# Windowed attention with a gated MLP behind it: q and k transposed on VectorE, scores as two 32-row products, one PSUM ring, and an instruction order written by a planner

## The chip, the cores and the metric

The kernel runs on one core of one Trainium2 chip. The metric is the device time of one launch in microseconds. Of the kernel before, three runs are known: 249.41, 250.86 and 250.92 us, median 250.86 us. The profile is of one execution, whose span from the first to the last instruction is 249.3 us.

## What is computed

Eight batches, eight heads, 576 tokens, 64 numbers a head, all fp32. Each token attends to itself and the 63 before it; the heads of a token laid side by side make a row of 512, which goes through a gated MLP whose gate is mixed over the tokens.

```python
scores = scale * np.matmul(q, k.transpose(0, 1, 3, 2))       # scale = 1/8
mask = (rel >= 0) & (rel < 64)                               # rel = query - key position
attn = softmax(np.where(mask, scores, -1e9))
x = np.matmul(attn, v)                                       # heads side by side: (8, 576, 512)
h = np.maximum(x @ w_in, 0.0)                                # w_in (512, 1024)
u, v = h[..., :512], h[..., 512:]
v_n = (v - mean(v)) / np.sqrt(var(v) + 1e-06)                # over the 512
v_s = np.einsum('ts,bsd->btd', w_spatial, v_n) + b_spatial   # over the 576 tokens
out = (u * v_s) @ w_out                                      # w_out (512, 512)
```

## The kernel before

**Stages of a batch.** Inputs are loaded as fp32 with the tokens on the partitions, in four chunks of 128 tokens and one of 64 (`load_heads`, `load_rem`, `load_chunk`, lines 68 to 76), so each descriptor moves one head's row of 256 bytes. GpSimd turns them into fp16 (lines 81 to 88; for batch 0 ScalarE and VectorE help) and copies v once more, shifted by 64 tokens (lines 93 to 106), so that any window of 128 keys starts on partition 0.

Attention goes in five steps `s` a batch: four pairs of heads over the tokens 0 to 511, and a fifth for the last 64 tokens of all heads ("the remainder"). In each:

- T (`emit_T`, lines 210 to 225): eight transposes on TensorE bring q and k of the pair to "numbers on the partitions", and VectorE copies the 128x1024 result from PSUM to `qk`.
- S (`emit_S`, lines 242 to 256): 16 matmuls make the scores, keys on the partitions, 64 keys against up to 192 queries. A head fills 64 rows of the array and 64 keys fill 64 columns, so four such tiles lie side by side in the array.
- E (`emit_E`, lines 264 to 270): ScalarE takes the exponential of 128x1024 scores, VectorE clips with the mask (a minimum with 0 or 65504).
- P (`emit_P`, lines 281 to 290): two matmuls with ones give the sums of the weights, 16 matmuls the products with v, both into `oz`.
- N (`emit_N1`, `emit_N2`, lines 298 to 308): ScalarE takes Ln and Exp(-x) of the sums, VectorE multiplies, which gives `x`, already transposed for the MLP.

The MLP of a batch has five units each of V (`emit_V`, lines 330 to 336: four matmuls of 512 columns, Relu on ScalarE, statistics on VectorE), U (lines 362 to 372), G (lines 382 to 394, the token mixing, five matmuls each) and O (lines 403 to 407: matmuls, a copy on ScalarE, a store), and one LN (lines 343 to 352) between V and G. The fifth unit of each is for the last 64 tokens; for V and O it takes as many matmuls of 512 columns as a full one (`pv_4`, `po_4`), in 64 of the array's 128 columns.

**PSUM** (eight banks): `tp` one bank, `sc` two, `oz` two, `mm` three for all MLP units.

**Order.** Every engine works its instructions strictly in program order, and the program order is written out by hand. `att_step` emits T of the next step, some MLP units, S of this step, P of the step before, then E and N with MLP units in between. A batch's attention runs beside the MLP of the batch before it; the lists `st[0]` to `st[4]` say which units go with which step. Batch 0 has no MLP beside it, and `warm` (line 114) fills TensorE with 16 and then four and three idle products at a time. The MLP of the last batch has no attention beside it. Loads go out on SyncE's queue one batch ahead, stores too from batch 2 on, in the same queue. The weights are loaded on GpSimd's queue, which turns them into fp16 on the way (lines 186 to 197).

Of the kernel before, what the change touches and what calls it, by code (L numbers as in the profile page):

```python
# [15 lines left out]
BIG = 65504.0  # L16


@with_exitstack
def kernel(  # L20
# [25 lines left out]
    inpool = ctx.enter_context(tc.tile_pool(name="inp", bufs=1))  # L46
    apool = ctx.enter_context(tc.tile_pool(name="attw", bufs=1))
    xpool = ctx.enter_context(tc.tile_pool(name="xt", bufs=1))
    mpool = ctx.enter_context(tc.tile_pool(name="moe", bufs=1))
# [3 lines left out]
    NAT = {}  # L53
    F16 = {}

    def new_batch(b):
        NAT[b] = [inpool.tile([128, 5, 8, 64], f32, tag=f"n{x}", bufs=2, name=f"n{x}{b}")
                  for x in "qkv"]

    def new_half(b):  # L60
        F16[b] = [inpool.tile([128, 5, 8, 64], f16, tag=f"h{x}", bufs=2, name=f"h{x}{b}")
                  for x in ("q", "k", "v", "s")]

    SRC = (q, k, v)

    def load_heads(b, x, h0, eng):
        for h in (h0, h0 + 1):
            eng.dma_start(NAT[b][x][:, 0:4, h, :],  # L68
                          SRC[x][b, h, 0:512, :].rearrange("(c p) d -> p c d", p=128))

    def load_rem(b, x, eng):
        eng.dma_start(NAT[b][x][0:64, 4, :, :], SRC[x][b, :, 512:576, :].transpose([1, 0, 2]))

    def load_chunk(b, x, c):
        sn = 128 if c < 4 else 64
        nc.sync.dma_start(NAT[b][x][0:sn, c, :, :],
                          SRC[x][b, :, 128 * c:128 * c + sn, :].transpose([1, 0, 2]))

    def cast_pair(b, x, p, eng):
        hs = slice(2 * p, 2 * p + 2)  # L80
        eng.tensor_copy(F16[b][x][:, 0:4, hs, :], NAT[b][x][:, 0:4, hs, :])  # L81

    def cast_rem(b, x, eng):
        eng.tensor_copy(F16[b][x][0:64, 4, :, :], NAT[b][x][0:64, 4, :, :])

    def cast_chunk(b, x, c, eng):
        sn = 128 if c < 4 else 64
        eng.tensor_copy(F16[b][x][0:sn, c, :, :], NAT[b][x][0:sn, c, :, :])  # L88

    def shift_pair(b, p, eng):  # L90
        hs = slice(2 * p, 2 * p + 2)
        vn, vs = F16[b][2], F16[b][3]
        eng.tensor_copy(vs[0:64, 0:4, hs, :], vn[0:64, 0:4, hs, :])
        eng.tensor_copy(vs[64:128, 1:5, hs, :], vn[64:128, 0:4, hs, :])

    def shift_rem(b, eng):
        eng.tensor_copy(F16[b][3][0:64, 4, :, :], F16[b][2][0:64, 4, :, :])

    def shift_half(b, half, eng):
        vn, vs = F16[b][2], F16[b][3]  # L100
        c = 2 * half
        if half < 2:
            eng.tensor_copy(vs[0:64, c:c + 2, :, :], vn[0:64, c:c + 2, :, :])
            eng.tensor_copy(vs[64:128, c + 1:c + 3, :, :], vn[64:128, c:c + 2, :, :])
        else:
            eng.tensor_copy(vs[0:64, 4, :, :], vn[0:64, 4, :, :])

    scratch = cpool.tile([128, 512], f16, name="scratch")
    nc.vector.memset(scratch[:], 0.0)  # L109

    def warm(n):
        t = psp.tile([128, 512], f32, tag="mm", bufs=3, name=f"warm{nc.next_id()}")
        for _ in range(n):
            nc.tensor.matmul(t[:, :], scratch[:, 0:128], scratch[:, :], start=True, stop=True)  # L114

    def load_by_pairs(b):
        new_batch(b)
        for p in range(4):
            for x in (1, 0, 2):
                load_heads(b, x, 2 * p, nc.scalar if (b == 0 and p < 2 and x == 2) else nc.sync)  # L120
        for x in (1, 0, 2):
            load_rem(b, x, nc.sync)
# [441 lines left out]
```

## Time and profile before

| | |
|---|---|
| runs | 249.41, 250.86, 250.92 us (median 250.86) |
| span of the profiled execution | 249.3 us, 0.1 us below the fastest run and 1.6 below the median |
| TensorE busy | 227.3 us, 91%, 2588 matmuls |
| VectorE, ScalarE, GpSimd busy | 155.3, 152.2, 122.1 us |
| mean granted TensorE clock | 0.962 of full speed |
| loads and stores | 40.41 MB, 120014 packets, 113776 of them under 512 bytes |

The page's slices cut the span into 40 parts of 6.2 us and give the busy share in tenths. The stage table gives for stretches of the span the busy microseconds of each engine (with the number of instructions), the granted clock, the busy share of the DMA engines and GB/s. In the timeline the columns are start, duration, engine, line, operation, tiles written and read, shapes and count, and in brackets how long the engine had been idle and for what. A matmul's duration includes the time to run through the array: the next one starts earlier, so prices below are taken from start to start. Line numbers are those of the code above.

### The profile page before, as it was taken

To read this page: it belongs to the slowest core of one execution; us is meant where nothing else is said; L and a number is where in the kernel's file an instruction comes from. 1 tells how busy PE (TensorE), PEld (TensorE's weight loads), DVE (VectorE), ACT (ScalarE), POOL (GpSimd) and SP (SyncE) were. 2 spreads that over 40 slices of the span, in tenths; PEclk is the share of its full clock that TensorE was granted. 3 is DMA by queue.
4 is the path that set the end of the run, shared out by engine and by line. 5 is a ranking of instruction groups with operands and counts; after the bars stand their busy time and mean duration, and the time that the engine had idled before them with its cause. 6 is when DMAs were issued, how large, how long until landed. Compare 5 with 4: busy or idle time off the path is not lost.

```text
span 249.3 us, 6391 instructions
## 1 busy us (share of the span) xinstructions
PE 227.3 (91%) x2588; PEld 116.8 (47%) x2588; DVE 155.3 (62%) x317; ACT 152.2 (61%) x266; POOL 122.1 (49%) x183
## 2 busy tenths in 40 slices
PE   7784996996399999999999999999999999999893
PEld 3442453553254464436544554455445544553351
DVE  6453277562459782887479556966597659755630
ACT  3373484446447666766785577756776677767423
POOL 3469638875499695369016592469135900000000
PEclk9999799799569999999999999999999999999998
DMA  8999999999999996992389948995499040014005
GB/s 159 218 184 208 216 204 229 191 201 276 249 199 210 198 178 175 246 206 52 128 192 211 192 128 221 189 198 135 137 216 156 27 165 5 3 42 149 0 3 189
DMA packets 120014, 40.41 MB, mean 162 GB/s; under 512 B 113776, under 2 KB 114864, under 8 KB 119984
## 3 DMA queue, kind: packets, MB, share of 16 engines
q1 hardware_dynamic: 114720, 34.88, 70.1%
q0 software_dynamic: 1840, 2.24, 5.2%
q10 hardware_dynamic: 3424, 2.88, 4.1%
q8 instruction: 20, 0.33, 0.6%
q14 instruction: 10, 0.08, 0.1%
HBM read 32.79 MB, written 9.44 MB: 169 GB/s over the span
## 4 chain that ended last, share of the span: by engine, by line
PE 60%; DVE 13%; ACT 9%; DMA 8%; SPq 3%; POOL 2%; issue 2%; ACTq 1%; POOLq 0%
SPq L68 3%; DMA nv_80<-in_v_dram 2%; DMA out_dram<-ob_0_1033 2%; DMA out_dram<-ob_1_3433 2%; DMA nq_78<-in_q_dram 2%; ACTq L407 1%; PE ps_0_804 L382 1%; PE warm_583 L114 1%; PE pv_0_1308 L330 1%; PE ps_0_4590 L382 1%; PE ps_0_4237 L382 1%; DVE mv_172 L336 1%; PE ps_0_3720 L382 1%; PE ps_1_895 L382 0%; PE ps_3_4653 L382 0%
## 5 line engine op out<-in xcount | busy, mean ns | idle before, releaser
L88 POOL CAST hq_2281<-nq_2285 128x512 f16<-128x512 f32 (+1 forms) x5 | 3.2, 635 | 12.8 <-DMA nq_2285<-in_q_dram 12.8
L114 PEld LDWEIGHTS <-scratch 128*128 128x128 f16 x51 | 5.0, 112 | 7.3 <-issue 3.8
L88 POOL CAST hq_3389<-nq_3393 128x512 f16<-128x512 f32 (+1 forms) x5 | 3.9, 797 | 8.8 <-DMA nq_3393<-in_q_dram 8.8
L281 PEld LDWEIGHTS <-onesK 128*64 128x64 f16 x80 | 4.6, 107 | 7.5 <-issue 5.2
L88 POOL CAST hq_2835<-nq_2839 128x512 f16<-128x512 f32 (+1 forms) x5 | 3.6, 720 | 8.3 <-DMA nq_2839<-in_q_dram 8.3
L176 ACT CAST hk_109<-nk_79 128x512 f16<-128x512 f32 x4 | 2.5, 618 | 7.5 <-DMA nk_79<-in_k_dram 7.5
L114 PE MATMUL warm_113<-scratch 128*128 128x512 f16 x16 | 5.5, 524 | 1.3 <-DVE scratch L109 1.3
L81 POOL CAST hv_110<-nv_80 128x512 f16<-128x512 f32 x4 | 2.5, 632 | 8.3 <-DMA nv_80<-in_v_dram 7.3
L88 POOL CAST hv_1729<-nv_1733 128x512 f16<-128x512 f32 (+1 forms) x5 | 3.5, 708 | 4.4 <-DMA nv_1733<-in_v_dram 4.4
L88 POOL CAST hq_1727<-nq_1731 128x512 f16<-128x512 f32 (+1 forms) x5 | 2.9, 609 | 4.6 <-DMA nq_1731<-in_q_dram 4.6
L88 POOL CAST hv_2283<-nv_2287 128x512 f16<-128x512 f32 (+1 forms) x5 | 3.2, 637 | 3.8 <-DMA nv_2287<-in_v_dram 3.8
L81 POOL CAST hv_433<-nv_437 128x512 f16<-128x512 f32 x4 | 2.5, 613 | 5.2 <-DMA nv_437<-in_v_dram 5.1
L88 POOL CAST hv_1184<-nv_764 128x512 f16<-128x512 f32 (+1 forms) x5 | 3.1, 611 | 3.9 <-DMA nv_764<-in_v_dram 3.9
L362 PEld LDWEIGHTS <-win_181 128*128 128x128 f16 x32 | 3.1, 98 | 3.8
L362 PEld LDWEIGHTS <-win_182 128*128 128x128 f16 x32 | 3.1, 98 | 3.8
L88 POOL CAST hv_1220<-nv_1224 128x512 f16<-128x512 f32 (+1 forms) x5 | 3.9, 780 | 2.0 <-DMA nv_1224<-in_v_dram 2.0
L88 POOL CAST hq_1182<-nq_762 128x512 f16<-128x512 f32 (+1 forms) x5 | 3.3, 654 | 3.2 <-DMA nq_762<-in_q_dram 2.7
L81 DVE CAST hq_108<-nq_78 128x512 f16<-128x512 f32 x4 | 1.7, 432 | 4.8 <-DMA nq_78<-in_q_dram 4.8
L281 PE MATMUL oz_3_1153<-e_1_3_1108,onesK 128*64 128x512 f16 x2 | 0.6, 611 | 4.4 <-DVE x_2_1133 L308 4.4
L88 POOL CAST hv_3391<-nv_3395 128x512 f16<-128x512 f32 (+1 forms) x5 | 3.0, 611 | 2.8 <-DMA nv_3395<-in_v_dram 2.8
L88 POOL CAST hv_2837<-nv_2841 128x512 f16<-128x512 f32 (+1 forms) x5 | 3.3, 666 | 2.0 <-DMA nv_2841<-in_v_dram 1.8
L264 ACT ACTIVATE e_1_0_831<-sc_0_813 128x1024 f16<-128x1024 f32 x1 | 1.0, 1023 | 5.2 <-PE sc_0_813 L242 5.2
(1871 smaller groups left out, 940.3 us busy)
## 6 DMA issues: line engine op xcount, KB each, us to landing
nk_79<-in_k_dram SPq DMA_DIRECT2D x9, 128.0 KB, 3.9
nq_78<-in_q_dram SPq DMA_DIRECT2D x9, 128.0 KB, 4.1
nk_436<-in_k_dram SPq DMA_DIRECT2D x9, 128.0 KB, 4.8
nq_435<-in_q_dram SPq DMA_DIRECT2D x9, 128.0 KB, 4.8
nv_437<-in_v_dram SPq DMA_DIRECT2D x9, 128.0 KB, 4.1
nk_763<-in_k_dram SPq DMA_DIRECT2D x4, 256.0 KB, 5.5
nq_762<-in_q_dram SPq DMA_DIRECT2D x4, 256.0 KB, 5.7
nv_764<-in_v_dram SPq DMA_DIRECT2D x4, 256.0 KB, 6.0
```

The source lines that it names most:

```text
L68: eng.dma_start(NAT[b][x][:, 0:4, h, :], SRC[x][b, h, 0:512, :].rearrange("(c p) d -> p c d", p=128))
L81: eng.tensor_copy(F16[b][x][:, 0:4, hs, :], NAT[b][x][:, 0:4, hs, :])
L88: eng.tensor_copy(F16[b][x][0:sn, c, :, :], NAT[b][x][0:sn, c, :, :])
L114: nc.tensor.matmul(t[:, :], scratch[:, 0:128], scratch[:, :], start=True, stop=True)
L176: nc.scalar.copy(o, i)
L264: nc.scalar.activation(e2[:, :, :], sc[:, :, :], AF.Exp, bias=0.0, scale=0.125)
L281: nc.tensor.matmul(oz[64 * h:64 * h + 64, 1, 0:n], onesK[:, :], e2[:, h, 0:n], start=True, stop=True)
L330: nc.tensor.matmul(pv[0:jn, :], xcol(b, r, j), w_in_sb[r][:, 512:1024], start=(r == 0), stop=(r == 3))
L336: nc.vector.bn_aggr(mv_t[b % NSB][0:jn, j, :], st6[0:jn, 0:6])
L362: nc.tensor.matmul(pu[:, :], w_in_sb[r][:, 128 * m:128 * m + 128], X[b, r][:, :], start=(r == 0), stop=(r == 3))
L382: nc.tensor.matmul(ps[:, :], VN[b, kk][0:kn, 128 * m:128 * m + 128], wspT[kk][0:kn, 0:512], start=(kk == 0), stop=(kk == 4))
L407: (nc.scalar if b < 2 else nc.sync).dma_start(out[b, 128 * j:128 * j + jn, :], ob[0:jn, :])
```

## The change

The kernel is rewritten around a list of steps with costs. What is computed stays the same.

- **q and k.** One contiguous load brings four heads of q or k: partition `32h + i` holds 18 tokens, 4608 bytes. They are cast to fp16 in one instruction of 128x1152. VectorE then transposes 32x32 blocks of 4-byte words, that is of pairs of fp16 numbers: 128x576 words, 4 instructions a batch. No transposes on TensorE and no copies of them from PSUM are left (40 transposes and 5 copies a batch).
- **Scores.** After the transpose a head fills 32 partitions, and each word holds two of the 64 numbers. S is made of two products of 32 rows each, summed in PSUM (`w` = 0 and 1), which read every other fp16 element. S now takes four heads at a time: 64 matmuls in place of two times 16; the remainder takes 32 matmuls in place of 16.
- **PSUM.** `tp` is gone. S of four heads takes both slots of a `ring` of two slots of two banks; each P takes one slot of the same ring. So S waits until both products P before it are normalized. `mm` has four banks in place of three.
- **64-token units.** V of the last 64 tokens and O of the last 64 tokens of the batch before go into one PSUM bank, in the two halves of the array's columns, with matmuls in turn.
- **Weights** are loaded as fp32 on SyncE's queue and cast by ScalarE, VectorE or GpSimd (17 loads, 17 casts). All loads and stores are on SyncE's queue. The idle products after the first 16 are gone.
- **v** is loaded by four heads (128 KB at a time, rows of 256 bytes as before), cast by two chunks, and shifted as before. From batch 2 on all casts and shifts are GpSimd's, as before.
- **Order.** Each step has an engine, a cost in us, the steps it depends on and the buffers it takes; the planner repeatedly takes the step that can start earliest by these costs (ties go to the lower key), and the instructions are emitted by planned start.

The core of the diff (the steps of MLP, weights and v are the same instructions in new functions):

```diff
+BUFS = {"nat": 5, "natv": 3, "hqk": 3, "qkT": 6, "hv": 4, "hs": 4, "e2": 3, "ring": 2, "mm": 4,
...
+AFTER = {"PE": 0.16, "ACT": 0.1, "DVE": 0.1, "POOL": 0.12, "DQ": 2.0}
+MODE_CHANGE = 0.095
-                for c in range(4):
-                    nc.tensor.transpose(tp[:, 512 + 128 * c:640 + 128 * c],
-                                        Kh[:, c, 2 * s:2 * s + 2, :], id16[:, :])
-                nc.vector.tensor_copy(qk[:, :], tp[:, :])
+            ld = add(f"ld{name}{b}_{g}", ("DQ", 1.55), key, lambda e: nc.sync.dma_start(
+                n.t[:, :], src[b, 4 * g:4 * g + 4, :, :].rearrange("h (i j) d -> (h i) (j d)", j=18)),
+                acq=[n])
+            c = add(f"c{name}{b}_{g}", engs, key, lambda e: cp(e, h.t[:, :], n.t[:, :]),
+                    deps=[ld], acq=[h], uses=[n])
+            d = add(f"t{name}{b}_{g}", ("DVE", 0.68), key, lambda e: nc.vector.transpose(
+                qt.t[:, :].rearrange("p (i j) -> p j i", j=18),
+                h.t[:, :].bitcast(f32).rearrange("p (j w) -> p j w", w=32)),
+                deps=[c], acq=[qt], uses=[h])
-                        nc.tensor.matmul(sc[r:r + 64, h, c0:c1],
-                                         qk[d, 512 + 64 * kap:576 + 64 * kap], qk[d, c0:c1],
-                                         start=True, stop=True)
+                for m in range(4):
+                    for w in (0, 1):
+                        for kap in (2 * m, 2 * m + 1):
+                            ...
+                            for hh in range(4):
+                                d = slice(32 * hh, 32 * hh + 32)
+                                nc.tensor.matmul(sc[hh // 2].t[r:r + 64, hh % 2, c0:c1],
+                                                 kT[d, 64 * kap:64 * kap + 64, w], qT[d, c0:c1, w],
+                                                 start=(w == 0), stop=(w == 1))
+        s = add(f"S{b}_{g}", ("PE", 0.5), key, emit_S, deps=[DKT[b, g], DQT[b, g], LASTP[0]],
+                acq=sc, uses=[KT[b, g], QT[b, g]], mode="s")
+            oz = buf("ring", f"oz{b}_{g}{u}")
+            p = add(f"P{b}_{g}{u}", ("PE", 0.5), key + 0.05, emit_P,
+                    deps=mins + DHV[b, g] + [prev], acq=[oz],
+                for r in range(4):
+                    nc.tensor.matmul(m.t[0:64, :], x4(b, r), w_in_sb[r][:, 512:1024],
+                                     start=(r == 0), stop=(r == 3))
+                    if prev is not None:
+                        nc.tensor.matmul(m.t[64:128, :], prev[0].t[:, 64 * r:64 * r + 64],
+                                         w_out_sb[r][:, :], start=(r == 0), stop=(r == 3))
```

In the order that the planner writes, TensorE's steps between the first S of batch 4 and that of batch 5 are: S (heads 0 to 3), V4 with O4 of the batch before, V2, V3, P, U0, P, U1, U2, U3, U4, S (heads 4 to 7), G0, G1, G2, P, G3, P, G4, O0, O1, S of the remainder, O2, O3, V0 of batch 4, P of the remainder, V1, V2. V, U, G and O up to there are those of batch 3. ScalarE's between the two exponentials of the first S and those of the second are: 3 Relus and a store copy, Ln, Relu, Exp, Ln, the LN's Ln, Exp, the LN's Exp, 3 Relus and the short Relu. In SyncE's queue the fifth v load of batch 0, heads 0 to 3, stands at place 17, behind 5 loads of q or k, 7 of v and 4 of weights; the fifth of batch 1, heads 4 to 7, at place 52, behind 12 loads of q or k, 21 of v and 18 of weights. A weight load waits until the cast of the second weight load before it has run (two buffers `wst`).

## The prediction

> **What bounds the kernel now.** I read the page's busy shares and slices first, then the stage table, then TensorE's timeline of one batch in the middle.
>
> ```profile
> PE 227.3 (91%) x2588; PEld 116.8 (47%) x2588; DVE 155.3 (62%) x317; ACT 152.2 (61%) x266; POOL 122.1 (49%) x183
> PE   7784996996399999999999999999999999999893
> DMA  8999999999999996992389948995499040014005
> ```
>
> TensorE is full from the eleventh slice on (62 us); no other engine is above 62%. The DMA engines are full for the first 16 slices only.
>
> ```profile
> 0.00:27.00 27.00, 19.52 (x234) 9.84 (x236) 13.25 (x50) 11.70 (x16) 17.17 (x37) 0.98 1.14 193
> 27.00:56.00 29.00, 26.96 (x276) 14.29 (x272) 17.22 (x31) 15.77 (x28) 19.65 (x32) 0.91 1.18 209
> 134.90:160.80 25.90, 25.38 (x314) 13.18 (x313) 18.50 (x36) 17.96 (x33) 13.83 (x20) 1.00 0.91 184
> 186.00:211.30 25.30, 25.30 (x314) 13.24 (x314) 18.19 (x35) 17.66 (x33) 9.77 (x12) 1.00 0.44 94
> ```
>
> The columns are PE, PEld, DVE, ACT, POOL, then clock, DMA share, GB/s. A batch in the middle takes about 26 us (first O at 92.71, 118.89, 144.97, 170.91, 196.68: mean 26.0), and TensorE is idle for under 1 us of it. What TensorE does there sets the time; about 56 us ahead of it and 40 us behind it are start and end. So I price TensorE's work from start to start:
>
> ```profile
> 117.08 0.41 PE L281 MATMUL oz_3_2228<-e_3_3_2143,onesK 128*64 128x512 f16 x2
> 117.32 0.23 PE L290 MATMUL oz_3_2228<-e_3_3_2143,hv_1220 128*64 128x64 f16 x4
> ...
> 117.67 0.20 PE L390 MATMUL ps_4_2251<-wspT_192,vn_0_1990 128*128 128x64 f16 x1
> ...
> 118.28 0.39 PE L210 MATMUL tp_1_2298<-id_130,hk_1728 128*128 128x128 f16 x4
> 118.51 0.39 PE L213 MATMUL tp_1_2298<-id_130,hq_1727 128*128 128x128 f16 x4
> 118.73 0.38 PE L403 MATMUL po_0_2310<-wout_183,g_0_2065 128*128 128x512 f16 x1
> ```
>
> ```profile
> 120.24 0.38 PE L403 MATMUL po_1_2319<-wout_186,g_3_2208 128*128 128x512 f16 x1
> 120.55 0.42 PE L242 MATMUL sc_0_2328<-qk_0_2191 64*64 64x128 f16 x16
> 120.90 0.30 PE L281 MATMUL oz_4_2346<-e2r_2248,onesK 128*64 128x256 f16 x2
> 121.03 0.29 PE L290 MATMUL oz_4_2346<-e2r_2248,hs_1221 128*64 128x64 f16 x8
> 121.25 0.39 PE L403 MATMUL po_2_2361<-wout_183,g_0_2065 128*128 128x512 f16 x1
> ```
>
> P takes 117.67 - 117.08 = 0.59, G4 0.61, T 0.45, S 0.35, P of the remainder 0.35; a matmul of 512 columns 0.215, so V, U or O 0.86 and G 1.08. The two `onesK` products in the two column halves take 0.24 together: they run side by side. U4 (16 products) takes 0.47, S of the remainder 0.25, T of the remainder 0.34, V4 and O4 0.98 each by the chain's pieces.
>
> **The change on TensorE, a batch in the middle.** Before: V 4 x 0.86 + 0.98 = 4.42, U 3.91, G 4.93, O 4.42, T 4 x 0.45 + 0.34 = 2.14, S 4 x 0.35 + 0.25 = 1.65, P 4 x 0.59 + 0.35 = 2.71; sum 24.2. The period is 26.0, so 1.8 go to gaps (0.09 between 120.46, the end of O1's streaming, and S, and about as much at every change of tile shape, some 19 a batch).
> - T: -2.14, all on the path. Its copies leave VectorE.
> - O4 beside V4: the `onesK` pair is the same shape, so both take 0.98: -0.98. If they ran in turn the gain would be 0.
> - S: 0.35 holds 0.1 of gap and 0.25 for four tiles of four products. Now there are eight tiles (four of 32 rows, two of 64 columns) of eight products: 2 x 0.25 + 0.1 = 0.6 for four heads if all eight run at once, 1.1 if four do, about 2 if reading every other element also halves the rate. No row shows 32-row tiles or this reading. I take 0.6, because the 64-row row shows tiles of both directions at once. The remainder: 2 x 0.15 + 0.1 = 0.4. S is then 1.6, with ends 1.5 and 4.7.
>
> After: V with O4 4.42, U 3.91, G 4.93, O 3.44, S 1.6, P 2.71 = 21.0, and 1.8 for gaps as before (17 changes of shape): **22.8 us a batch** against 26.0.
>
> The 0.09 gap is the row for the change of shape. The Trainium skill, "TensorEngine Tiling (Array Packing)", Key Properties, says that changing the tiling mode drains TensorE; that speaks against a third shape of tile, 32 by 64. By the row the drains stay at 1.8 a batch; if a 32-row drain cost twice that of the row, the batch would be 0.5 longer.
>
> No row shows a strided operand. The skill, "SBUF — State Buffer", under Door 1, says that strides up to 8 bf16 elements are free; by it the reading adds nothing.
>
> **Other engines, a batch.** VectorE is busy 18.5 of 25.9. It loses five copies (4 x 0.67 + 0.41 = 3.1) and gains four transposes. The nearest row is a 512-element product from PSUM, 0.69; times 576/512 that is 0.75, so 3.0 in all; the slowest clip (1.32 for 1024 elements) makes an upper end of 1.5 each, 6.0, and 21.4 busy, still under 22.8. Hidden. ScalarE: the same operations and one more short exponential (0.38): 18.4, hidden. GpSimd: 4 casts of 1152 at 0.65 x 1152/512 = 1.5, 4 of v at 0.65, 8 shifts at 0.61 and 2 of half that: 14, hidden. DMA: a 256-byte packet takes 22.5 ns in the trace's packet records, a 2-KB one 92.6, so q and k (1.67 us for 590 KB on 16 engines) 6.7, v 6.5, stores 3.3: 16.5 in place of 22.7, hidden. What hides all four is TensorE's 22.8; each us by which one of them passes it is a us of the period, six to the end. The 17 casts of weights (0.55 each, on three engines, 3 us) lie beside the loads of the start; uncovered they are 3 us once.
>
> **The start.** No wait of TensorE sets it, but the queue of loads: 128 KB of v take 0.72, 256 KB of weights 0.74. Heads 0 to 3 of batch 0 need the load at place 17: 5 x 1.67 + 7 x 0.72 + 4 x 0.74 + 0.36 = 16.7, and with 0.85 to the first issue and 2 to land 19.5. Today the first P is at 12.1, for one pair. From there the ring (below, 7.8 us for four heads, 3.5 for the remainder): first V about 31 (today 30.15), S of batch 1 about 36. Heads 4 to 7 of batch 1 need place 52: 12 x 1.67 + 18 x 0.72 + 3 x 0.36 + 12 x 0.74 + 4 x 0.83 + 0.4 = 47, so 50. P, normalization, remainder, V0 and O0 to O2 bring S of batch 2 to about 61. Two delays come on top: weight loads wait for casts that stand behind the first X on VectorE, and without idle products the clock falls as it does today in 26 to 28 us (0.50). I add 3: **64**, ends 56 (loads all ahead) and 74 (two of these waits in a row).
>
> **The end.** From S of batch 7 on TensorE has S 1.6, P 2.71, V 4 of batch 6 with V3 1.84, U, G, O of batch 6 12.28, then V, U, G, O of batch 7 17.7: 36.1, gaps 1.8, 0.7 at the last LN, and 3.9 from the last matmul to the end (245.4 to 249.3 today): 42.5.
>
> Sum: 64 + 5 x 22.8 + 42.5 = 220.5, against the execution's 249.3. The median of the runs lies 1.5 above that: **222**.
>
> **Rivals.**
> - The ring binds; this one can end slower. Its chain, by start-to-start rows: S to exponential 0.85, two exponentials 2.07, clip 0.79, P to Ln 0.70 (117.08 to 117.78), Ln, Exp, Ln, Exp 2.56, product 0.79: 7.8 for four heads, 19.0 a batch with the remainder. That is under 22.8, if nothing stands in between. But ScalarE's other work (15 instructions of about 0.55 and the LN, 8.8) and VectorE's (11.8) are in the same strict queues. If all of ScalarE's falls into the chain, the period is 27.8. The time is 85.2 + 6 x period (64 + 42.5 - 22.8 + 1.5, and six periods), so it is above 250.9 from 27.6 on; with a quarter of VectorE's as well (2.9) the period is 30.7 and the time 269. For it: today's `sc` and `oz` are separate and S never waits for a product; a late S now holds back all that stands behind it on TensorE (G0 to G2, U or V), and with them their Relus. Against it: the written order has 2.6 to 4 us of MLP on TensorE at each step of the chain.
> - The ring binds in part: period 25.5, 238.
> - S does not pack, or reads at half rate: 1.1 each, 0.7 for the remainder, 24.1 a batch and 230; both, 26.9 and 247.
> - The loads hide what TensorE saves, or the order slips everywhere: no change, from a period of 27.2 to 28.0 (248.4 to 253.4).
>
> **How the numbers follow.** The forecast 0.60, its own range 210 to 230 by the ends of the start; S 0.10; ring in part 0.16; ring in full, slower, 0.11; no change 0.03. The first three make faster by over 1% 0.86 (1% is about what a measurement of this kernel can tell from no change); same 0.03, slower 0.11. The range reaches from the start's lower end and 0.3 less gap a batch, 207, to the ring in part with a late start, 240.
>
> **What would show it.** Right: no idle TensorE in the middle slices, 22 to 23.5 us from first O to first O, S about 0.6, transposes under 0.9, first V near 31. Wrong: TensorE idle ahead of S with a VectorE product named as releaser (the ring); S over 1 (packing); SyncE or DMA named ahead of P after 60 us (loads).

## The result, and the profile after

The changed kernel takes **230.69 us** (median of 4 runs, 230.07 to 231.10) against 250.89 us for the kernel before in the same runs: ratio 0.918 (95% interval 0.914 to 0.923). The forecast was 222, with 207 to 240 as the range, so direction and range hold. The likeliest case was 8.7 us too low and its own range of 210 to 230 is missed by 0.7. Ratios here compare undisturbed runs only, so one can differ a little from the quotient of two medians.

The page's parts 1 and 2 of the changed kernel:

```profile
PE 193.3 (85%) x2873; PEld 98.1 (43%) x2873; DVE 178.6 (78%) x341; ACT 157.1 (69%) x281; POOL 84.1 (37%) x124
PE   7413329886989997999899997999799999999993
PEclk9955556998899999999999999999999999999999
DMA  6999889799988999979689728511310041014005
```

TensorE's busy time fell by 34 us, but the span only by 20.9 (249.3 to 228.4): TensorE's share is down from 91 to 85%, VectorE's up from 62 to 78%. Slices 3 to 6 (11 to 34 us) are 10 to 30% busy at a clock of a half, and in the middle a 7 or an 8 stands between the 9s about once a batch. The stage table, cut where S of batches 2 to 7 starts (PE, PEld, DVE, ACT, POOL, clock, DMA share, GB/s):

```profile
69.30:93.70 24.40, 22.79 (x359) 11.60 (x358) 19.72 (x35) 18.48 (x34) 16.56 (x23) 1.00 0.96 288
93.70:116.70 23.00, 21.50 (x356) 10.92 (x355) 19.23 (x33) 17.39 (x32) 13.72 (x20) 1.00 0.87 227
116.70:141.00 24.30, 23.00 (x367) 11.67 (x366) 21.33 (x37) 18.48 (x34) 13.03 (x19) 1.00 0.71 204
141.00:163.90 22.90, 21.43 (x351) 10.93 (x350) 20.18 (x33) 17.39 (x32) 12.96 (x19) 1.00 0.37 120
163.90:186.90 23.00, 22.94 (x367) 11.71 (x369) 18.27 (x35) 18.36 (x34) 5.74 (x10) 1.00 0.16 54
```

Each of the first four stages holds 1.3 to 1.6 us in which TensorE does nothing (length less PE); the fifth, where VectorE no longer has transposes to do, holds none. (The stages alternate in length because the plan puts five full V units into one and three into the next.)

| | forecast | measured |
|---|---|---|
| first S of batch 1 | about 36 | 41.07 |
| first S of batch 2 | 64 | 69.25 |
| period in the middle | 22.8 | 24.49, 22.95, 24.28, 22.95, 22.94: mean 23.5 |
| from S of batch 7 (186.86) to the end | 42.5 | 41.5 |
| span | 220.5 | 228.4 |
| median of the runs above it | 1.5 | 2.3 |

So +5.25 at the start, +3.6 in five periods, -1.0 at the end, +0.8 outside the span: 8.7. Two things had to be explained: 5 us of start, which are there at S of batch 1 already (from there to S of batch 2 it is 28.2 us for 28, where the forecast's 28 hold its 3 us for delays), and 0.7 us a batch.

For the middle, the first view is what TensorE waits for:

```profile
PE sc L366 <- DVE x L413: 8.0, 7, 3.5
PE ozr L453 <- DVE e_r L444: 6.2, 5, 1.6
PE oz L389 <- DVE e L377: 6.1, 2, 4.2
```

(total us, times, longest.) The waits of S for a product (`sc`, the ring) all lie before 53 us, but for one of 0.2 us at 102.1, and those for `e` lie before 28 us. The wait in the middle is `ozr`: P of the remainder waits for the remainder's clip. VectorE's timeline shows why that clip is late:

```profile
134.90 1.26 DVE L306 STREAM_TRANSPOSE kT<-hk 128x576 f32<-128x576 f32 x1 [0.78 <-PE scr L430]
136.00 1.24 DVE L306 STREAM_TRANSPOSE qT<-hq 128x576 f32<-128x576 f32 x1
137.08 1.24 DVE L306 STREAM_TRANSPOSE kT<-hk 128x576 f32<-128x576 f32 x1
138.16 0.57 DVE L444 TENSOR_TENSOR e_r<-e_r,maskr 128x512 f16<-128x512 f16 x1
```

The exponential of the remainder is done at 135.7; the clip runs at 138.16 because three transposes for later batches stand in front of it. They take 1.25 us (spaced 1.09), not 0.75; and the first of them could not start earlier, because it waits for S of the remainder to release its buffer (`scr` as releaser). TensorE, which has only so much MLP work written between S and P of the remainder, stands still:

```profile
138.78 0.30 PE L453 MATMUL ozr<-e_r,onesK 128*64 128x256 f16 x2 [1.30 <-DVE e_r L444]
```

The four middle waits are 1.61, 1.31, 1.30 and 1.30: 5.5 us, 1.1 a batch over the five periods. Taken off, they leave 23.5 - 1.1 = 22.4, a little under the 22.8 that TensorE's units were added up to. (This is a subtraction; no run below reaches it.)

**Theory after the result:** the 0.7 us a batch is a block of VectorE, dear transposes in front of a clip on the path; the 5 us of start are SyncE standing still for the two staging buffers of the weights (in the first 40 us it issues nothing for 2.2 to 3.8 us five times, each time ahead of a weight load) and TensorE's half clock. **Rivals:** S is dearer than forecast because of its strided reading; the pair O4/V4 does not pay; the chain through the ring is the true limit and the rest only fills its holes; for the start, the clock alone, or a chain through VectorE that no earlier load can shorten.

### The profile page after: what moved, and what is told of

It is laid out like the page before. It is cut to its first block, busy times and chain, and to the rows that moved or that the text cites. A ratio compares the mean times of both kernels' runs of the same rounds, so it can differ in the third digit from the quotient of the medians.

```text
span 228.4 us, 6947 instructions
## 1 busy us (share of the span) xinstructions
PE 193.3 (85%) x2873; PEld 98.1 (43%) x2873; DVE 178.6 (78%) x341; ACT 157.1 (69%) x281; POOL 84.1 (37%) x124
## 2 busy tenths in 40 slices
DMA packets 50417, 42.67 MB, mean 187 GB/s; under 512 B 39569, under 2 KB 39569, under 8 KB 50386
## 3 DMA queue, kind: packets, MB, share of 16 engines
q1 hardware_dynamic: 50386, 42.23, 62.8%
## 4 chain that ended last, share of the span: by engine, by line
PE 54%; DVE 17%; DMA 13%; ACT 8%; issue 4%; SPq 1%; POOL 0%; DVEq 0%; ACTq 0%; POOLq 0%
PE pg L589 16%; PE pv L506 8%; PE po L614 7%; PE pu L559 6%; DMA nq<-in_q_dram 6%; DVE qT L306 4%; PE sc L366 4%; DMA ws<-in_moe_w_spatial_dram 4%; DVE kT L306 3%; PE oz L389 3%; PE oz L394 2%; ACT e L374 2%; DMA wi<-in_moe_w_in_dram 2%; PE pg L595 2%; DMA wo<-in_moe_w_out_dram 2%
## 5 line engine op out<-in xcount | busy, mean ns | idle before, releaser
L219 POOL COPY hs<-hv 64x512 f16<-64x512 f16 x51 | 33.8, 665 | 25.1 <-ACT hv L217 10.6
L589 PE MATMUL pg<-wspT,vn 128*128 128x512 f16 (+1 forms) x160 | 39.4, 389 | 1.0 <-DVE vn L543 1.0
L374 ACT ACTIVATE e<-sc 128x1024 f16<-128x1024 f32 x32 | 31.1, 1022 | 4.3 <-PE sc L366 3.6
L506 PE MATMUL pv<-win,x 128*128 128x512 f16 x128 | 32.6, 395 | 0.0
L603 DVE TENSOR_TENSOR g<-pg,ru 128x512 f16<-128x512 f32 (+1 forms) x40 | 24.7, 634 | 9.1 <-PE pg L589 9.1
L377 DVE TENSOR_TENSOR e<-e,mask 128x1024 f16<-128x1024 f16 x32 | 26.8, 854 | 5.7 <-ACT e L374 5.7
L559 PE MATMUL pu<-x,win 128*128 128x512 f16 x128 | 31.0, 380 | 0.0
L614 PE MATMUL po<-wout,g 128*128 128x512 f16 x128 | 30.5, 380 | 0.0
L488 DVE BATCH_NORM_STATS2 st<-vs 128x6 f32<-128x512 f16 (+1 forms) x40 | 26.9, 677 | 4.1 <-ACT vs L486 3.8
L486 ACT ACTIVATE vs<-pv 128x512 f16<-128x512 f32 (+1 forms) x40 | 23.5, 594 | 6.7 <-PE pv L506 5.5
L411 ACT ACTIVATE zi<-ln 128x512 f32<-128x512 f32 (+1 forms) x40 | 23.7, 593 | 0.9
L306 DVE STREAM_TRANSPOSE kT<-hk 128x576 f32<-128x576 f32 x16 | 20.0, 1250 | 3.6 <-PE scr L430 3.2
L589 PEld LDWEIGHTS <-vn 128*128 128x128 f16 (+1 forms) x160 | 13.9, 98 | 17.7 <-DVE vn L543 4.8
```

The lines of the kernel that those rows point to most:

```text
L219: ENG[e].tensor_copy(o, i)
L306: d = add(f"t{name}{b}_{g}", ("DVE", 0.68), key, lambda e: nc.vector.transpose(qt.t[:, :].rearrange("p (i j) -> p j i", j=18), h.t[:, :].b ...
L374: ex = add(f"E{b}_{g}{u}", ("ACT", 0.91), key, lambda e, u=u: nc.scalar.activation(e2[u].t[:, :, :], sc[u].t[:, :, :], AF.Exp, bias=0.0, s ...
L377: mins.append(add(f"M{b}_{g}{u}", ("DVE", 0.58), key, lambda e, u=u: nc.vector.tensor_tensor(e2[u].t[:, :, :], e2[u].t[:, :, :], mask[:, : ...
L411: c = add(f"n{b}_{r}", ("ACT", 0.09 + 0.0008 * n), key, lambda e: nc.scalar.activation(zi.t[:, 0:n], lz.t[:, 0:n], AF.Exp, bias=0.0, scale ...
L486: rl = add(f"Vr{b}_{j}", ("ACT", 0.5), key, lambda e: nc.scalar.activation(vs.t[0:jn, :], m.t[0:jn, :], AF.Relu), deps=[pv], acq=[vs], use ...
```

## The experiments

### The middle: what the transposes cost

**A contiguous write.** Each 32x32 block goes to 32 adjacent words instead of words 72 bytes apart. The tokens of q and k then stand in a permuted order, so the scores are not those of the reference; the work is the same.

```diff
-                qt.t[:, :].rearrange("p (i j) -> p j i", j=18),
+                qt.t[:, :].rearrange("p (j i) -> p j i", j=18),
```

> VectorE's transposes write their result in one run in place of every 18th word; the tokens then stand in another order, so the scores are those of other pairs of tokens. Every instruction keeps its place. Theory A: the write in steps of 72 bytes makes the transpose 1.25 us; it falls to 0.7 to 0.8, VectorE loses 32 x 0.5 = 16 us, the start and the waits at the remainder shrink, and the time falls by 4 to 8 us to 223 to 227. Theory B: the transposition of 4-byte words itself runs at this rate, the row stays at 1.25 and the time within 1 us.

Measured: 227.49 us (226.45 to 229.18), ratio 0.908 (0.903 to 0.914). A group line of this run (x instructions, then busy us, mean ns of one, idle time ahead of them and what ended it), and below it the same group from the page of the changed kernel:

```profile
L306 DVE STREAM_TRANSPOSE kT<-hk 128x576 f32<-128x576 f32 x16 | 12.2, 763 | 3.5 <-PE scr L430 3.2 <-ACT hk L217 0.3
```

```profile
L306 DVE STREAM_TRANSPOSE kT<-hk 128x576 f32<-128x576 f32 x16 | 20.0, 1250 | 3.6 <-PE scr L430 3.2
```

763 against 1250 ns: the forecast's 0.75 (taken from a product, not a transpose) happens to be the price of a contiguous write, and the step of 72 bytes adds 0.5 us to each of 32 transposes. VectorE is busy 167.0 us for 178.6, the `ozr` waits fall from 6.2 to 2.7 us in all, the mean period from 23.5 to 23.0, and S of batch 2 starts at 69.3 as before. Of 11.6 us less work on VectorE, 2.5 us reach the span (225.9), all of them in the periods: the middle `ozr` waits are 2.8 us shorter (5.5 to 2.7), the five periods 2.6. So the length of the transposes accounts for 0.5 of the 0.7 us a batch. The gain stays under the 4 to 8 us of theory A, and not only because the start does not move: in three of the middle batches the remainder's clip now takes 1.33 us where it took 0.57 (111.66, 135.47 and 157.93 us), about as much as the wait of 0.82 us that is left in each. Why it does is not shown.

**Smaller steps with the reference's token order.** If a partition holds not one run of 18 tokens but nine runs of 2, or three runs of 6, the step of the write is 8 or 24 bytes; the rows of the loads shrink from 4608 to 512 or 1536 bytes. (The transposes' output is arranged to match; the diff shows runs of 2, where runs of 6 have 384 and 6.)

```diff
-            ld = add(f"ld{name}{b}_{g}", ("DQ", 1.55), key, lambda e: nc.sync.dma_start(
-                n.t[:, :], src[b, 4 * g:4 * g + 4, :, :].rearrange("h (i j) d -> (h i) (j d)", j=18)),
+            def ldq(e):
+                for hh in range(4):
+                    nc.sync.dma_start(
+                        n.t[32 * hh:32 * hh + 32, :].rearrange("p (o r) -> p o r", r=128),
+                        src[b, 4 * g + hh, :, :].rearrange("(o i r) d -> i o (r d)", i=32, r=2))
```

> Tokens go to partitions in pairs (a partition holds tokens 64 o + 2 i and the one after) in place of 18 in a run: loads of q and k in rows of 512 bytes, four loads where there was one, and transposes that write steps of 8 bytes in place of 72. Order as before, the result is the reference's. Theory: the write's step sets the transposes' 1.25 us (1.25 to 0.76 when it wrote in one run); at 8 bytes it is under 0.9, and VectorE gains 11 us or more; the loads cost more (rows of 512 bytes, 64 loads more on SyncE's queue), which shows in the start only: 227 to 230. Rival: the loads lose more in the start than the transposes give: 231 or above.

> Six tokens in a run: the loads of q and k read rows of 1536 bytes (4 DMAs each), the transposes write with a step of 24 bytes where it was 72. If a step of 24 bytes is written like one of 8: transposes 0.76 us, periods mean 23.0 as with the contiguous write, and about 227.5 us, unless the smaller rows cost what rows of 512 bytes did. If 24 bytes cost like 72: 1.25 us each, and 230 to 232 us. If the loads bind: q1 well over 70% and waits of the casts on loads.

Measured: runs of 2 tokens 263.4 us (261.85 to 263.9), ratio 1.046 (1.039 to 1.054); runs of 6 tokens 254.1 us (252.44 to 254.86), ratio 1.011 (1.007 to 1.016). The first is slower than the kernel before, the second by about 1%. The page's packets and load queue (packets, MB, share of the 16 engines) with 8-byte steps, and the group of transposes there:

```profile
DMA packets 84724, 42.69 MB, mean 163 GB/s; under 512 B 41106, under 2 KB 77970, under 8 KB 84691
q1 hardware_dynamic: 84690, 42.24, 81.4%
```

```profile
L310 DVE STREAM_TRANSPOSE kT<-hk 128x576 f32<-128x576 f32 x16 | 12.3, 766 | 4.5 <-PE scr L434 3.2 <-ACT hk L217 1.3
```

The same from the page of the run with 24-byte steps:

```profile
DMA packets 60147, 42.69 MB, mean 170 GB/s; under 512 B 41105, under 2 KB 53393, under 8 KB 60114
q1 hardware_dynamic: 60114, 42.24, 77.2%
L310 DVE STREAM_TRANSPOSE kT<-hk 128x576 f32<-128x576 f32 x16 | 19.4, 1212 | 4.2 <-PE scr L434 2.4
```

8 bytes are written as fast as in one run (0.77 us), 24 almost as slowly as 72 (1.21). This agrees with the rule that the prediction applied to TensorE's reading and not to VectorE's writing: the Trainium skill, "SBUF — State Buffer", Door 1, says that the memory works in lines of 16 bytes, that full rate needs two accesses to a line, and that steps up to 4 fp32 or 8 bf16 elements are free. A step of 8 bytes is 2 of these words, 24 bytes are 6 and 72 are 18. (No run here shows 16 bytes.)

The loads ate more than the transposes gave. The queue's same 42.2 MB in 84690 or 60114 packets in place of 50386 raise its share of the 16 DMA engines from 62.8% to 81.4 and 77.2% of a longer span, and TensorE's waits grow: with runs of 6, S waits 18.3 us for products (8.0 after the change), once 9.2 us at a stretch, and DMA makes up 51% of the chain of waits (13% after the change). These runs also issue four loads for one, so packet size and number of loads are not told apart. They do show that the gain of the change depends on how q and k are loaded: with short rows and four loads for one, in the same order, the new kernel is no faster than the old.

### The middle: order or amount

**The remainder's clip ahead of the transposes.** After the planner has run:

```diff
+    at = {o.name: i for i, o in enumerate(order)}
+    for b in range(B - 1):
+        i, j = at[f"S{b}_r"], at[f"M{b}_r"]
+        span = order[i:j + 1]
+        late = [o for o in span if o.name[:2] in ("tk", "tq")]
+        order[i:j + 1] = [o for o in span if o not in late] + late
```

> After the planner has run, the remainder's clip (M) is moved ahead of the transposes that stand between the remainder's S and that clip on VectorE; these transposes are for later batches, nothing else moves. Theory (the long periods come from P of the remainder waiting for a clip that stands behind three transposes): the 6.2 us of waits at ozr fall to about 2, P of the remainder starts about 1.3 us earlier in the long periods, the periods of 24.3 to 24.5 fall to about 23.2, and the kernel is 3 us faster, near 227.5 us. Rival (VectorE has no room, so the transposes behind the clip make the clips or x of the next batch late by as much): the waits move to sc and oz and the time stays at 230.7.

Measured: 232.05 us (229.73 to 233.81), ratio 0.923 (0.918 to 0.927): not faster than the change. The rival held. TensorE's and VectorE's timelines of this run, same batch:

```profile
136.34 0.30 PE L453 MATMUL ozr<-e_r,onesK 128*64 128x256 f16 x2
...
138.53 0.24 PE L366 MATMUL sc<-qT,kT 32*64 32x128 f16 x2
140.35 0.76 PE L366 MATMUL sc<-qT,kT 32*64 32x128 f16 x62 [1.58 <-DVE x L413]
```

```profile
134.67 0.42 DVE L444 TENSOR_TENSOR e_r<-e_r,maskr 128x512 f16<-128x512 f16 x1 [1.62 <-ACT e_r L440]
135.01 1.25 DVE L306 STREAM_TRANSPOSE kT<-hk 128x576 f32<-128x576 f32 x1
...
138.27 1.24 DVE L306 STREAM_TRANSPOSE qT<-hq 128x576 f32<-128x576 f32 x1
139.35 0.63 DVE L488 BATCH_NORM_STATS2 st<-vs 128x6 f32<-128x512 f16 x1
139.90 0.40 DVE L413 TENSOR_TENSOR x<-ozr,zi 128x256 f16<-128x256 f32 x1
```

P of the remainder starts 2.96 us behind S of the remainder (133.38) in place of 4.33, and waits for nothing, as planned. But now the same block of four transposes (135.01 to 139.4) stands in front of the remainder's product `x`, and the next S, which needs the ring slot that this product frees, waits 1.58 us. The wait has moved one link down the chain, at no lower a price: in the five periods these waits are 6.5 us for 5.5, and the mean period is 23.9 for 23.5. (The profile is of the execution of 229.73 us, the shortest; in it S of batch 2 starts at 66.62 for 69.25, which covers the longer periods. Why it starts earlier was not looked into.)

**The transposes behind that product too.** The same loop with `X{b}_4` in place of `M{b}_r`, on top of the nine staging buffers and the idle products described below (that kernel alone: 228.86 us).

```diff
-        i, j = at[f"S{b}_r"], at[f"M{b}_r"]
+        i, j = at[f"S{b}_r"], at[f"X{b}_4"]
```

> The kernel of the run before with nine staging buffers and the idle products, and now the transposes that stand between the remainder's S and the remainder's x on VectorE are all moved behind that x, so that they delay neither the remainder's clip nor the x that the next S waits for. Theory (a block of four transposes, 4.3 us of VectorE, in the middle of the chain from the remainder's S to the next batch's S is all that separates the long periods from the short): no wait over 0.5 us is left at ozr and at the first S of a batch from batch 3 on; the five periods fall from a mean of 23.55 to about 23.0; S of batch 7 starts near 182.4 and the median is about 226 us. Rival (VectorE has no hole for 4.3 us anywhere, so the block now makes the next batch's clips, or its transposes for the second S, late): the waits turn up at oz or at the second S with 1 to 2 us each, the mean period stays at 23.5, and the time at 229 us.

Measured: 245.59 us (244.32 to 247.0), ratio 0.978 (0.973 to 0.984). The theory that this order is what was wrong fell. No wait is left at `ozr` or at the first S, but:

```profile
148.01 0.42 DVE L414 TENSOR_TENSOR x<-ozr,zi 128x256 f16<-128x256 f32 x1
148.35 1.25 DVE L307 STREAM_TRANSPOSE kT<-hk 128x576 f32<-128x576 f32 x1
...
151.60 1.24 DVE L307 STREAM_TRANSPOSE qT<-hq 128x576 f32<-128x576 f32 x1
...
154.30 1.67 DVE L378 TENSOR_TENSOR e<-e,mask 128x1024 f16<-128x1024 f16 x2
```

```profile
155.02 0.41 PE L390 MATMUL oz<-e,onesK 128*64 128x512 f16 x2 [2.70 <-DVE e L378]
...
156.83 0.64 PE L390 MATMUL oz<-e,onesK 128*64 128x512 f16 x2
```

```profile
152.00:156.00 4.00, 1.30 (x22) 0.78 (x21) 3.93 (x9) 1.94 (x4) 3.88 (x5) 1.00 0.88 316
156.00:160.00 4.00, 4.00 (x27) 1.61 (x26) 2.92 (x7) 2.96 (x8) 3.76 (x7) 0.57 0.54 145
```

These are VectorE's timeline, TensorE's timeline and the stage table of this run. Now the clips of the next batch's four heads stand behind the block (148.35 to 152.7) and behind three statistics of V that it has pushed back (152.72 to 154.2), and P waits 2.70 us for them. In the stretch after that the granted clock is 0.57, and the second P and the U units behind it run at about half speed: TensorE is busy 23.6 us a batch in place of 22.3. The mean period is 26.4 us. So three places for the block have been tried on the chip: in front of the clip (1.3 us of waiting), in front of the product (1.0 to 1.6), in front of the next clips (2.0 to 2.7, and the clock). What was not tried is to scatter the four transposes one by one between links of the chain.

**A truer cost in the planner.** The planner's cost of a transpose is set from 0.68 to the measured spacing, and it plans again.

```diff
-            d = add(f"t{name}{b}_{g}", ("DVE", 0.68), key, lambda e: nc.vector.transpose(
+            d = add(f"t{name}{b}_{g}", ("DVE", 1.09), key, lambda e: nc.vector.transpose(
```

> The planner is told 1.09 us for a VectorE transpose in place of 0.68 (1.09 is the spacing of two in a row in the trace of the changed kernel), and plans anew. Theory: in two of the middle batches the clip of the remainder waits behind three transposes and holds P of the remainder back 1.3 us; with the right cost the planner moves them, and the periods of 24.4 us come to 23: 2 to 4 us less, 227 to 229. Rival (the ring binds, whatever the order): periods as before, within 1 us of 230.7.

Measured: 245.47 us (244.12 to 251.26), ratio 0.977 (0.971 to 0.984): the opposite. The profile is of the execution of 251.26 us, with a span of 249.2; the other three have 242.0 to 244.6, so the sizes read from it are too large for them. The waits, and S of heads 4 to 7 of batch 4:

```profile
PE sc L366 <- DVE x L413: 23.7, 16, 2.8
```

```profile
136.12 0.24 PE L366 MATMUL sc<-qT,kT 32*64 32x128 f16 x2 [1.57 <-DVE x L413]
137.36 0.76 PE L366 MATMUL sc<-qT,kT 32*64 32x128 f16 x62 [1.00 <-DVE x L413]
```

The new order puts S of heads 4 to 7 directly behind the second P of heads 0 to 3: U1 to U4, which stood between them, are done ahead of that P. Little then covers the ring, and S waits 2.6 to 3.2 us in each of the batches 2 to 6; the mean period is 26.3, and S of batch 2 starts 7.2 us later than after the change. The five longer periods (13.9 us) hold TensorE's stretches of half clock too. This is the prediction's rival "the ring binds in part" (25.5, 238), made real by an order, and more than it: the chain through the ring is a limit close by, and it is the MLP units between its links that hide it. One true cost in a plan whose other costs are off (S 0.5 for 0.70, clip 0.58 for up to 1.6) did not give a better plan.

### TensorE's savings

**S with contiguous reading.** Each product reads a contiguous half of the 64 numbers' words instead of every other element; the pairs are then the wrong ones, so the scores are not the reference's.

```diff
-        return t[:, :].bitcast(f16).rearrange("p (t w) -> p t w", w=2)
+        return t[:, :].bitcast(f16).rearrange("p (w t) -> p t w", w=2)
```

> S reads the first and the second half of each transposed row (every element) in place of the even and the odd elements; the products then mix tokens, so the scores are not the reference's. Theory: reading every other element costs nothing, S stays at 0.70 us for four heads, time within 1 us of 230.7. Rival: it costs part of the rate; S falls to 0.5, 0.5 us a batch less, 227.

Measured: 231.74 us (229.91 to 232.41), ratio 0.923 (0.918 to 0.928); S 0.68 to 0.70 us, as with the strided reading. In S, reading every other element costs nothing that shows, and S's 0.70 for the forecast's 0.6 is not due to it.

**O4 behind V4 instead of in turn.** Four products of V4, then four of O4.

```diff
-                    if prev is not None:
-                        nc.tensor.matmul(m.t[64:128, :], prev[0].t[:, 64 * r:64 * r + 64],
-                                         w_out_sb[r][:, :], start=(r == 0), stop=(r == 3))
+                for r in range(4 if prev is not None else 0):
+                    nc.tensor.matmul(m.t[64:128, :], prev[0].t[:, 64 * r:64 * r + 64],
+                                     w_out_sb[r][:, :], start=(r == 0), stop=(r == 3))
```

> The four products of O4 follow the four of V4 in place of standing between them; everything else keeps its place. Theory: two column halves only run side by side if their products come in turn; the eight take 0.215 each, the unit grows from 0.99 to 1.85 us, 0.86 in each of seven batches, all on TensorE's path: 6 us more, 236 to 237. Rival: column halves overlap wherever they stand, or the ring and not TensorE sets the period: within 1 us of 230.7.

Measured: 230.74 us (229.82 to 232.83), ratio 0.920 (0.911 to 0.929): no change. TensorE's timeline of this run, V4 (L518) and O4 (L521):

```profile
117.02 0.40 PE L518 MATMUL pv<-win,x 128*64 128x512 f16 x1
117.03 0.40 PE L521 MATMUL pv<-wout,g 128*64 128x512 f16 x1
117.26 0.38 PE L518 MATMUL pv<-win,x 128*64 128x512 f16 x1
117.27 0.38 PE L521 MATMUL pv<-wout,g 128*64 128x512 f16 x1
```

The kernel's text has four L518 and then four L521; the records show the first of each starting 0.01 us apart. The two column halves overlap even so, and the unit is 0.99 us either way. The pairing counts, the turns in the kernel's text do not.

**The pair alone, in the kernel before.** O4 of batches 1 to 6 goes into the free half of V4 of the next batch.

```diff
                                  start=(r == 0), stop=(r == 3))
+                if j == 4 and b > 1:
+                    nc.tensor.matmul(pv[64:128, :], G[b - 1, 4][:, 64 * r:64 * r + 64],
+                                     w_out_sb[r][:, :], start=(r == 0), stop=(r == 3))
```

> The kernel before with this one part of the change: O4 of batches 1 to 6 stands in turn with V4 of the next batch in one bank (batches 0 and 7 as before). Theory: 0.98 us off TensorE's path six times: 5 to 6 us less than the kernel before, ratio 0.976 to 0.981. Rival: V4, which now waits for the product G4 of the batch before and ScalarE's second copy, costs as much as it saves: ratio 0.995 to 1.005.

Measured: 246.61 us (246.46 to 247.03), ratio 0.981 (0.975 to 0.987); the span falls by 4.3 us, 0.7 for each of six pairs where 0.98 of TensorE's work goes. Shown: this part of the change alone is worth about a fifth of it. Why 0.3 of each pair does not arrive stays open. How the other four fifths divide between the transposes that left TensorE, the fourth `mm` bank, the new loads and the planner's order was not measured one by one.

### The start

**Nine staging buffers for the weights** instead of two (of 576 words each for 1024).

```diff
+        n = 9 if tag == "wst" else BUFS[tag]
-        return Buf(tag, lambda: pool.tile(shape, d, tag=tag, bufs=BUFS[tag], name=name))
+        return Buf(tag, lambda: pool.tile(shape, d, tag=tag, bufs=n, name=name))
```

> Nine staging buffers for the weights in memory in place of two; the planner still counts with two, so that every instruction keeps its place. Theory: in the start SyncE's queue stands still ahead of weight loads (2.3, 2.3, 2.2, 3.8, 0.7 and 2.7 us in the trace of the changed kernel) because the cast that frees the buffer stands behind attention work on VectorE or ScalarE, and with it all loads behind. Part of it is covered by loads in flight: S of batch 2 moves from 69.3 to about 65, and the time falls by 3 to 6 us to 225 to 228. Rival: VectorE's own work (57 us busy in the first 69) sets the start, and the time falls by less than 1.5 us.

Measured: 228.71 us (225.59 to 230.28); the ratio of 0.904 (0.897 to 0.911) rests on the two shortest executions, 225.59 and 227.54 us, which lie within the theory's 225 to 228. The profile is of the longest (230.28 us, span 228.1), which gains nothing; the two shortest have spans of 223.4 and 225.4 and no profile, so where they gain is not known. In the profile S of batch 1 starts at 38.56 for 41.07, but S of batch 2 at 69.20 for 69.25. Its stage table shows one place where the 2.5 us go:

```profile
50.00:54.00 4.00, 2.19 (x65) 0.95 (x64) 4.00 (x8) 2.85 (x5) 3.16 (x5) 0.85 0.78 211
54.00:58.00 4.00, 3.99 (x25) 1.58 (x25) 2.54 (x5) 1.23 (x2) 3.39 (x4) 0.50 0.99 289
58.00:62.00 4.00, 4.00 (x37) 1.86 (x36) 2.37 (x4) 1.23 (x2) 0.00 (x0) 0.79 0.68 151
```

TensorE arrives at G of batch 0 too early and stands idle while VectorE is busy all four microseconds (50 to 54), most of them with the five `vn` that G needs: 3.69 us here (51.05 to 54.7), 1.69 after the change. Then it works the next eight at a clock of 0.50 and 0.79 (0.61 and 0.96 after the change).

**Idle products, without and with the staging buffers.** 59 products of 512 columns with no use, behind eight steps of the start, to hold the clock up.

```diff
+        if o.name in IDLE:
+            t = psp.tile([128, 512], f32, tag="mm", bufs=BUFS["mm"], name="idle_" + o.name)
+            for _ in range(IDLE[o.name]):
+                nc.tensor.matmul(t[:, :], scratch[:, 0:128], scratch[:, :], start=True, stop=True)
...
+IDLE = {"S0_0": 12, "P0_00": 4, "P0_01": 10, "S0_1": 8, "P0_11": 14, "S0_r": 2, "U0_4": 6, "S1_1": 3}
```

> Idle products of 512 columns (59 in all) stand on TensorE at eight places of batches 0 and 1 where it waits, after S or P, as the kernel before had them; every other instruction keeps its order. Theory: the granted clock of 0.50 between 22 and 37 us and 0.61 at 54 to 58 goes to 1.0, V0 to V2 and the first G run at full rate, and S of batch 2 comes 2 to 4 us earlier: 227 to 229. Rival: the idle products stand in the way of the ring, or VectorE sets the start: within 1 us of 230.7 or above.

> Nine staging buffers for the weights and the 59 idle products of before, together. If the 2.5 us that nine staging buffers won at the first S of batch 1 were lost again to TensorE's granted clock of 0.50 at 54 to 58 us: S of batch 2 starts near 67, time 227 to 228 us. If S of batch 2 is set by the chain ring, VectorE and remainder's clip in batch 1: it stays at 69.2, and the time is 229 to 231 us whatever the clock.

Measured: idle products alone 231.41 us (230.06 to 232.7), ratio 0.920 (0.913 to 0.927), S of batch 2 at 69.8: a clock of 1.00 from 23 us on gives nothing by itself. With nine buffers 228.86 us (227.4 to 230.72), ratio 0.912 (0.907 to 0.917): S of batch 1 at 37.23 and S of batch 2 at 67.44. So 3.8 us of the 5 that S of batch 1 was late are staging buffers and clock together, but only 1.8 of them reach S of batch 2. Where the rest may be held shows in the chain of waits of this last run between 36 and 68 us:

```profile
by line: DVE hs L220 9.0%; DVE vn L544 8.7%; issue 8.1%; DVE qT L307 7.5%; PE pg L590 7.5%; PE pu L560 5.7%; DVE x L414 5.1%; PE wps L267 5.0%; DVE g L604 4.9%; PE oz L390 4.1%; DVE st L489 4.1%; ACT zi L412 3.9%; DVE kT L307 3.4%; ACT ln L
```

It runs through VectorE's shifts of v (`hs`), `vn`, transposes and products more than through TensorE (42.7% against 22.3% in the pieces listed). That points to VectorE, but lighter transposes alone (the contiguous write) left S of batch 2 at 69.3, and other work on VectorE there was not made lighter. Of the two with nine buffers, the interval of the buffers alone (0.897 to 0.911) lies just below the change's (0.914 to 0.923), and the one with idle products (0.907 to 0.917) overlaps it: a gain of about 1%, hardly more than can be told apart.

## Why the prediction was right, and where it failed

**Right: what carries the gain.** TensorE's units were added up to 22.8 us a batch from rows of the kernel before; less the clip's wait the period is 22.4, and TensorE's mean busy time in the five periods is 22.3. The pair came at 0.99 (0.98), P at 0.59, the remainder's S at 0.27 (0.4). S packs: 0.70 for 0.6, so the rival "S does not pack, or reads at half rate" is out by the row and by the experiment on reading. The third shape of tile cost nothing beyond the row of 0.09: the last matmul of V starts at 93.43 and streams for 0.215, and S starts at 93.74, 0.095 behind it. ScalarE (17.4 to 18.5 us in the stage table for 18.4) and GpSimd (13.0 to 16.6 while it has casts, for 14) were sized right, and hidden. So was DMA over the whole span: 62.8% of 228.4 is 143 us, for 8 x 16.5 and some 13 for the weights; the loads run ahead, so the stages hold from 0.96 x 24.4 = 23.4 down to 3.7. The end was 41.5 for 42.5.

**Wrong: "VectorE hidden".** The step compared VectorE's busy time per batch, 21.4 at the upper end of its price, with TensorE's 22.8, and called it hidden. The price itself went to that side: 1.25 us, between the chosen 0.75 and the upper end of 1.5. But even so VectorE is busy only 18.3 to 21.3 us a batch, never more than TensorE. What failed is the test. VectorE is in the chain from S of the remainder to the P behind the next S with three links (clip, product, next clip), it works in program order, and ahead of each of the three a block of transposes (3.3 us in the change, 4.3 in the two runs that moved it) made TensorE wait 1.0 to 2.7 us a batch. "Each us by which one of them passes it" was the wrong bound; by these three runs the better one is the longest block that stands ahead of a link, less the cover that TensorE has written between the two ends of that link. Two of the prediction's own signs of being right, no idle TensorE in the middle slices and transposes under 0.9, did not appear.

**Wrong: the start, 64 for 69.25.** The load queue was priced by bytes, and from there on the ring by its bare chain (7.8 us and 3.5), plus 3 us for waits of weight loads and for the clock. The load at place 17 was to land at 19.5, and VectorE starts on it at 19.82; but P of heads 0 to 3 does not wait for it and starts at 13.86. The first V comes later than forecast (34.63 for 31): from first P to first V it is 20.8 us where the forecast had 11.5. That is the step that failed, the ring's chain in the start; that the early P takes 5.6 off these 9.3 us is luck. In this stretch S of heads 4 to 7 of batch 0 waits 3.5 and 2.0 us for products and S of the remainder 3.9 and 0.3. VectorE's timeline of the changed kernel shows what stands ahead of these products:

```profile
21.11 0.76 DVE L219 CAST hq<-nq 128x1152 f16<-128x1152 f32 x1 [1.01 <-DMA nq<-in_q_dram]
21.79 0.68 DVE L413 TENSOR_TENSOR x<-oz,zi 128x512 f16<-128x512 f32 x1
...
32.56 0.46 DVE L219 CAST wnat<-ws 128x576 f16<-128x576 f32 x1 [1.17 <-DMA ws<-in_moe_w_spatial_dram]
32.93 1.28 DVE L413 TENSOR_TENSOR x<-oz,zi 128x512 f16<-128x512 f32 x2
```

ScalarE has their factor `zi` ready at 19.45 and, for the last two, at 30.48 and 31.63; the products stand behind casts that wait for loads, and SyncE issued these two loads (at 14.90 and 29.17) behind standstills of 2.3 and 3.8 us. Of the delays, buffers and clock, for which the 3 us stood, are worth 3.8 at S of batch 1 (41.07 to 37.23) and 1.8 at S of batch 2 (69.25 to 67.44); what the rest would be worth no run tells. The ends of 56 and 74 held it.

**Sums of the prediction that do not come out.** With S at its upper end (4.7 for 1.6) the period is 25.9 and the time 241, not 26.9 and 247. The start's ends of 56 and 74 by themselves give 214 and 232, not 210 and 230, and the terms named for the whole range give 212 and 248, not 207 and 240; the result lies inside all of these but 210 to 230. The times listed for the first O of a batch are each 0.16 us later than in TensorE's timeline (118.89 for 118.73), which leaves the period as it is.

**The rivals.** "The ring binds in full" did not happen, since in the middle no S waits more than 0.2 us; "in part" is true of the first 53 us (8.0 us of waits, and 4.2 more of S of the remainder), and one change of a planner's cost made it true of batches 2 to 6 at 245.5. What keeps it out is the order. That the 1.1 us a batch could be had by another order, and not only moved along the chain, no run shows.

## What to carry to other kernels

An engine that is less busy than the bound is not thereby hidden: look for the links of the chain that stand in its queue, and for the longest block of other work ahead of one. Price a strided write by its step and not only by its elements, and check whether a layout that makes the write cheap makes the loads dear; here long rows in single loads were worth more than fast transposes. A planner's order is one of several near its own optimum: a truer cost or a sensible swap can lose 15 us, so each order has to be measured.

## What the hardware showed that was not expected

- 32x32 transposes of 128x576 4-byte words on VectorE: 0.76 us with a contiguous write, 0.77 with a step of 8 bytes, 1.21 with 24, 1.25 with 72.
- Products in the two column halves of TensorE's array overlap even when four of one half stand ahead of four of the other in the kernel's text (starts 0.01 us apart).
- VectorE's fp16 clips of 128x1024, 0.69 us mostly, take up to 1.6 (in the change two in 3.18 us from 118.56 on, two in 1.28 from 55.62 on), and five `vn` 3.69 with nine staging buffers in place of 1.69 in the change, at moments when GpSimd is busy. No run tells whether GpSimd is the cause.
- After 2.7 us of idle TensorE (152.3 to 155.0 us) in the run with the transposes moved furthest, the granted clock was 0.57 in the stretch from 156 to 160 us, and 1.00 before.
